# A tile's first and second attention units: values and place moved behind the next unit's scores time, in a bank of the h products

## The chip, the cores and the metric

The kernel runs on one core of a Trainium2 chip. Its time is the device time of one execution in microseconds (us). Engines: TensorE (PE, with its weight loads PEld), VectorE (DVE), ScalarE (ACT), GpSimd (POOL) and SyncE (SP), which issues nearly all transfers.

## The reference

Three layers on float32 data, 3072 tokens (4 batches of 768) of width 512 (8 heads of 64):

```python
# attention by chunks of 32 queries: 16 keys to the left, 8 to the right, and 8 memory keys
scores = scale * np.matmul(q_c, k_full.transpose(0, 1, 3, 2))
scores = scores - np.max(scores, axis=-1, keepdims=True)
a = np.exp(scores)
a = a / (np.sum(a, axis=-1, keepdims=True) + 1e-09)
out[:, :, c_start:c_end] = np.matmul(a, v_full)
# x = the heads side by side, [3072, 512]
h = x @ w_in                                              # 512 -> 2048
g = np.maximum(h, 0.0) + np.log1p(np.exp(-np.abs(h)))     # softplus
x = g @ w_out                                             # 2048 -> 512
out = ((x @ w_a) * (x @ w_b)) @ w_out2                    # 512 -> 1536 -> 512
```

## The kernel before, in words

**Stage 1** makes attention and the softplus layer, in 8 tiles (t = 0 to 7) of 384 tokens, about 74 us each, from 49 to 628 us of the span. A tile has 16 steps f, one for each 128 of the 2048 hidden columns. A step is `emit_h` (12 matmuls of 128x384 into a PSUM tile `ph`, tag "h", two banks), `emit_soft` (ScalarE Abs, Exp, Ln into `e`; VectorE `g`, L558, the last reader of `ph`; ScalarE and GpSimd split g into `gh` and `gl`), and `emit_x1` of the step two before (12 matmuls into four accumulators `px`, which hold four banks). Matmul inputs are split in a high and a low part, so a product takes three matmuls.

**Attention of tile t+1** is woven into tile t, in three units of 128 tokens (`Unit`, UPT = 3). A unit's steps: `turn` (VectorE transposes `kn`, `qn` into `kt`, `qt`), `scores` (32 small matmuls into two PSUM tiles `sc`, tag "att", two banks), `soft` and `norm` (softmax), `flip` and `flip2` (VectorE transposes the weights into `af`), `values` (32 small matmuls `pxa` of `af` with the values tile `vn`, one bank, tag "att"; the first 16 use the first half of the 128 queries, the rest the second), `place` (ScalarE copies `pxa` into the tile's x, VectorE subtracts for the low part). Tile 7 has no attention woven in.

**What sets the order.** `plan` is a list of (time, unit, step). Tile t has 32 times, two to an f: `att_at(slot)` is called behind `emit_h` and behind `emit_x1`, and pops each step whose time is at most the slot. A unit's `values` and `place` come at its time `at` less 0.1 and `at`; the others earlier, by STEPS (FIRST_STEPS for a tile's first unit, EARLY_STEPS for the three units woven into tile 0). In tiles 1 to 6 the program order is kept on TensorE, VectorE and SyncE; ScalarE and GpSimd are ordered by a scheduler.

**Loads.** There is one values tile (SETS = 1): the load for the next unit (`load_v`, two to five transfers on SyncE in pieces of 256 bytes) can start when the `values` before have read it. `Loaded.fetch` brings `kn` and `qn` of the tile after, in four parts (36 transfers, rows of 128 bytes), once the last unit of a tile has been turned. SyncE's other transfers in these tiles are weights on their way to scratch memory (`raw_*`, `v_scratch`) and results of the tile (`x_scratch`). All go out in the order of the program on one queue.

Stage 2 (628 to 1175 us) is the gated layer; the diff does not touch it.

Of the kernel before, what the change touches and what calls it, by code (L numbers as in the profile page):

```python
# [9 lines left out]
F32 = mybir.dt.float32  # L10
# [15 lines left out]
SETS = 1  # L26
# [24 lines left out]
def attn_moe_moe2(ctx: ExitStack, tc: tile.TileContext, q, k, v, mem_k, mem_v,  # L51
# [7 lines left out]
    P = 128  # L59
# [6 lines left out]
    UPT = TT // QU  # L66
# [4 lines left out]
    KT = DM // P  # L71
# [6 lines left out]
        name=nc.get_next_instruction_name(), act_func_set_id=6, ins=[], outs=[]))  # L78
# [8 lines left out]
    ps = ctx.enter_context(tc.tile_pool(name="ps", bufs=2, space=PSUM))  # L87
# [18 lines left out]
    class Weight:  # L106


        def __init__(self, dst, key):
            self.dst, self.key = dst, key  # L110
# [199 lines left out]
    class Block:  # L310
# [48 lines left out]
        def values(self):  # L359
            self.px = px = self.psum(4, "pxb")[:, :KT * QB].rearrange("p (i t) -> p i t", i=KT)  # L360
            for i in range(KT):
                for j in range(2):
                    r = slice(64 * j, 64 * j + 64)
                    nc.tensor.matmul(px[r, i], lhsT=self.vn[:, 2 * i + j, :], rhs=self.af[:, i, r], start=True, stop=True)
# [28 lines left out]
    class Unit:  # L393


        def __init__(self, u):
            self.u = u
            self.b, self.n = divmod(u, NU)

        def load_v(self):  # L400
            self.v = vsets[self.u % SETS]
            self.v.fetch(self.b, self.n)
# [66 lines left out]
        def values(self):  # L469
            u = self.u  # L470
            vn = self.v.v
            self.px = px = ps.tile([P, 512], F32, tag="att", name=f"pxa{u}").rearrange("p (i t) -> p i t", i=KT)

            for w in range(2):
                for i in range(KT):
                    for j in range(2):
                        nc.tensor.matmul(px[64 * j:64 * j + 64, i, QB * w:QB * w + QB], lhsT=vn[:, w, 2 * i + j],  # L477
                                         rhs=af[:, 2 * w:2 * w + 2, KT * j + i], start=True, stop=True)
# [18 lines left out]
    blocks = [Block(u) for u in range(BPT)]  # L497
    units = [Unit(u) for u in range(B * NU)]

    plan = []  # L500
    for i, unit in enumerate(units[UPT:]):
        at = 2 * NF1 * (i + 1) // UPT - START + NEXT_LATER * (i == EARLY) - (i % UPT == UPT - 1)
        steps = FIRST_STEPS if i % UPT == 0 else STEPS
        if i < EARLY:
            steps = EARLY_STEPS[i]
            at = steps[-1][0]
        plan += [(at + d - steps[-1][0], i, getattr(unit, step)) for d, step in steps]
        if i < SETS:
            plan.append((2 + i, -1, unit.load_v))
        if i + SETS < len(units[UPT:]):  # L510
            plan.append((at + 1, i, units[UPT + i + SETS].load_v))
        if i % UPT == UPT - 1 and unit.u + 1 < len(units):
            turned = at + steps[0][0] - steps[-1][0]
            plan += [(turned + 1 + part, i, partial(loaded.fetch, unit.u // UPT + 1, part)) for part in range(KT)]
# [549 lines left out]
```

## Time and profile before

| | us |
|---|---|
| median of 3 runs (lowest, highest) | 1179.31 (1178.32, 1180.07) |
| the profiled execution | 1176.61 |
| its span | 1174.8 |
| TensorE busy | 1165.4 |
| VectorE, ScalarE, GpSimd busy | 725.7, 532.2, 264.8 |

The span runs from the first to the last instruction of the profiled execution; the rest of its time lies around the span. A share of the whole span mixes the two stages, so the stretches of single tiles say more: tile t of stage 1 lies at 49 + 74 t to 123 + 74 t, roughly. Starts of matmuls on TensorE's timeline are exact, their ends are modelled and overlap the next start, so costs there are read from start to start.

### The profile page before, as it was taken

To read this page: it belongs to the slowest core of one execution; us is meant where nothing else is said; L and a number is where in the kernel's file an instruction comes from. 1 tells how busy PE (TensorE), PEld (TensorE's weight loads), DVE (VectorE), ACT (ScalarE), POOL (GpSimd) and SP (SyncE) were. 2 spreads that over 40 slices of the span, in tenths; PEclk is the share of its full clock that TensorE was granted. 3 is DMA by queue.
4 is the path that set the end of the run, shared out by engine and by line. 5 is a ranking of instruction groups with operands and counts; after the bars stand their busy time and mean duration, and the time that the engine had idled before them with its cause. 6 is when DMAs were issued, how large, how long until landed. Compare 5 with 4: busy or idle time off the path is not lost.

```text
span 1174.8 us, 20105 instructions
## 1 busy us (share of the span) xinstructions
PE 1165.4 (99%) x7462; PEld 1048.8 (89%) x7462; DVE 725.7 (62%) x1603; ACT 532.2 (45%) x1293; POOL 264.8 (23%) x239
## 2 busy tenths in 40 slices
PE   9899999999999999999999999999999999999998
PEld 6799999999999999999999888888888888888887
DVE  6888654556545665456377667867456657545555
ACT  6799666656566566665565332222211113111110
POOL 2000322323223222232233665721002101000000
PEclk9999999999999999999999999999999999999999
DMA  9965334353443534442374758464864443864301
GB/s 230 281 206 105 96 102 109 102 103 88 107 94 120 104 88 107 93 121 66 122 259 162 291 215 286 169 225 140 334 214 146 151 145 99 309 225 153 137 1 72
DMA packets 191154, 181.45 MB, mean 154 GB/s; under 512 B 120609, under 2 KB 149201, under 8 KB 191057
## 3 DMA queue, kind: packets, MB, share of 16 engines
q1 hardware_dynamic: 190672, 180.12, 49.2%
q8 instruction: 59, 0.97, 0.3%
q14 instruction: 39, 0.31, 0.1%
q0 software_dynamic: 384, 0.05, 0.0%
HBM read 129.79 MB, written 50.33 MB: 153 GB/s over the span
## 4 chain that ended last, share of the span: by engine, by line
PE 95%; DMA 2%; SPq 1%; ACT 0%; DVE 0%; issue 0%
PE px L571 23%; PE ph L547 22%; PE py L779 17%; PE pX L756 8%; PE pW L756 8%; PE pV L756 8%; PE pY L756 4%; PE pxa L477 2%; PE sc L430 1%; DMA kp<-in_k_dram 1%; DMA raw<-in_moe_w_in_dram 1%; SPq L331 1%; SPq L328 0%; PE sc L305 0%; PE pa L466 0%; SPq L102 0%
## 5 line engine op out<-in xcount | busy, mean ns | idle before, releaser
L547 PE MATMUL ph<-x,w 128*128 128x384 f32 x1536 | 289.7, 336 | 0.1
L571 PE MATMUL px<-gh,w 128*128 128x384 f32 x1024 | 283.2, 337 | 0.0
L547 PEld LDWEIGHTS ph<-x,w 128*128 128x128 f32 x1536 | 266.7, 188 | 2.2 <-issue 0.3
L779 PE MATMUL py<-w2o,c 128*128 128x512 f32 (+1 forms) x870 | 218.0, 388 | 0.0
L558 DVE SCALAR_TENSOR_TENSOR g<-ph,e 128x384 f32<-128x384 f32 x128 | 71.3, 557 | 206.3 <-ACT e L556 205.9
L779 PEld LDWEIGHTS py<-w2o,c 128*128 128x128 f32 x870 | 162.7, 188 | 33.5
L571 PEld LDWEIGHTS px<-gh,w 128*128 128x128 f32 x1024 | 186.7, 188 | 2.4 <-issue 0.2
L571 PE MATMUL px<-gl,w 128*128 128x384 f32 x512 | 171.2, 334 | 0.0
L838 ACT CAST c<-r 128x512 fp32r<-128x512 f32 x36 | 22.4, 621 | 308.2 <-DVE r L836 287.2
L538 POOL TENSOR_TENSOR gl<-g,gh 128x384 fp32r<-128x384 f32 x96 | 98.9, 1030 | 243.4 <-ACT gh L535 216.5
L554 ACT ACTIVATE e<-ph 128x384 f32<-128x384 f32 x128 | 62.2, 486 | 105.1 <-PE ph L547 91.0
L788 DVE TENSOR_TENSOR y<-py,y 128x512 f32<-128x512 f32 (+1 forms) x121 | 82.9, 685 | 36.2 <-PE py L779 36.0
L535 ACT CAST gh<-g 128x384 fp32r<-128x384 f32 x128 | 65.7, 513 | 73.8 <-DVE g L558 72.6
L571 PEld LDWEIGHTS px<-gl,w 128*128 128x128 f32 x512 | 96.1, 188 | 0.1
L448 DVE STREAM_TRANSPOSE af<-sm 32x256 f32<-32x256 f32 x180 | 78.2, 434 | 2.5
L555 ACT ACTIVATE e<-e 128x384 f32<-128x384 f32 x128 | 67.3, 526 | 4.0
L556 ACT ACTIVATE e<-e 128x384 f32<-128x384 f32 x128 | 67.3, 526 | 3.8
L835 DVE TENSOR_TENSOR d<-pW,q 128x512 f32<-128x512 f32 x36 | 24.9, 691 | 69.1 <-PE pW L756 69.1
L384 ACT ACTIVATE sm<-sm,st 128x96 f32<-128x96 f32 x168 | 60.5, 362 | 3.6 <-DVE st L380 3.6
L756 PE MATMUL pX<-x,u 128*128 128x512 f32 x216 | 54.8, 389 | 0.0
L756 PE MATMUL pW<-xs,u 128*128 128x512 f32 x216 | 54.8, 389 | 0.0
L756 PE MATMUL pY<-xs,u 128*128 128x512 f32 x216 | 54.8, 389 | 0.0
(162 smaller groups left out, 1636.7 us busy)
## 6 DMA issues: line engine op xcount, KB each, us to landing
u<-u_scratch SPq DMA_DIRECT2D x72, 512.0 KB
u_scratch<-u SPq DMA_DIRECT2D x36, 512.0 KB
w2o<-w2o_scratch SPq DMA_DIRECT2D x24, 512.0 KB
raw<-in_moe_w_in_dram SPq DMA_DIRECT2D x16, 512.0 KB
raw<-in_moe_w_out_dram SPq DMA_DIRECT2D x16, 512.0 KB
vn<-in_v_dram SPq DMA_DIRECT2D x35, 176.0 KB
raw_a<-in_moe_w_a_dram SPq DMA_DIRECT2D x12, 512.0 KB
raw_b<-in_moe_w_b_dram SPq DMA_DIRECT2D x12, 512.0 KB
```

The source lines that it names most:

```text
L448: nc.vector.transpose(out=af[32 * kb:32 * kb + 32, x], in_=self.sm[32 * x:32 * x + 32, :, 32 * kb:32 * kb + 32])
L535: anchor[0] = nc.scalar.copy(hi, val)
L538: engine.tensor_tensor(lo, val, hi.bitcast(F32), ALU.subtract)
L547: nc.tensor.matmul(ph, lhsT=w[:, a, kt * P:(kt + 1) * P], rhs=x[:, c, kt, :], start=n == 0, stop=n == 3 * KT - 1)
L554: nc.scalar.activation(e, ph, AF.Abs)
L555: nc.scalar.activation(e, e, AF.Exp, scale=-1.0)
L556: nc.scalar.activation(e, e, AF.Ln, bias=1.0)
L558: nc.vector.scalar_tensor_tensor(g, ph, 0.0, e, ALU.max, ALU.add)
L571: nc.tensor.matmul(acc[t][i][:, :TT], lhsT=a, rhs=c, start=f == 0 and m == 0, stop=f == NF1 - 1 and m == 2)
L756: nc.tensor.matmul(bank[:, :T2], lhsT=u[:, j, a, kt * P:kt * P + P], rhs=x[kt][:, c], start=first_ and m == 0, stop=m == 3 * KH - 1, skip_ ...
L779: nc.tensor.matmul(b, lhsT=c[:, x, r], rhs=w[:, y, cols], start=n == 0, stop=n == 3 * GROUP - 1)
L788: tt(y, b, y, ALU.add)
```

## The change

For a tile's first and second unit (i % UPT 0 and 1) `values` and `place` leave the unit's own times and take times just ahead of the next unit's `scores` (0.02 and 0.01 earlier). Their `pxa` comes from tag "h" in place of "att". The load of the next unit's values, which must follow, moves from `at + 1` to `at + 3` for these units. A tile's last unit keeps its times, its bank and `at + 1`.

```diff
--- before.py
+++ after.py
@@ -396,6 +396,7 @@
         def __init__(self, u):
             self.u = u
             self.b, self.n = divmod(u, NU)
+            self.own_bank = False
 
         def load_v(self):
             self.v = vsets[self.u % SETS]
@@ -469,7 +470,7 @@
         def values(self):
             u = self.u
             vn = self.v.v
-            self.px = px = ps.tile([P, 512], F32, tag="att", name=f"pxa{u}").rearrange("p (i t) -> p i t", i=KT)
+            self.px = px = ps.tile([P, 512], F32, tag="h" if self.own_bank else "att", name=f"pxa{u}").rearrange("p (i t) -> p i t", i=KT)
 
             for w in range(2):
                 for i in range(KT):
@@ -497,18 +498,23 @@
     blocks = [Block(u) for u in range(BPT)]
     units = [Unit(u) for u in range(B * NU)]
 
-    plan = []
+    plan, scored = [], {}
     for i, unit in enumerate(units[UPT:]):
         at = 2 * NF1 * (i + 1) // UPT - START + NEXT_LATER * (i == EARLY) - (i % UPT == UPT - 1)
         steps = FIRST_STEPS if i % UPT == 0 else STEPS
         if i < EARLY:
             steps = EARLY_STEPS[i]
             at = steps[-1][0]
-        plan += [(at + d - steps[-1][0], i, getattr(unit, step)) for d, step in steps]
+        whens = [(at + d - steps[-1][0], step) for d, step in steps]
+        scored[i] = dict((step, a) for a, step in whens)["scores"]
+        if i % UPT and i > 0:
+            plan += [(scored[i] + d, i - 1, getattr(units[UPT + i - 1], step)) for d, step in ((-0.02, "values"), (-0.01, "place"))]
+            units[UPT + i - 1].own_bank = True
+        plan += [(a, i, getattr(unit, step)) for a, step in whens if step not in ("values", "place") or i % UPT == UPT - 1]
         if i < SETS:
             plan.append((2 + i, -1, unit.load_v))
         if i + SETS < len(units[UPT:]):
-            plan.append((at + 1, i, units[UPT + i + SETS].load_v))
+            plan.append((at + 1 if i % UPT == UPT - 1 else at + 3, i, units[UPT + i + SETS].load_v))
         if i % UPT == UPT - 1 and unit.u + 1 < len(units):
             turned = at + steps[0][0] - steps[-1][0]
             plan += [(turned + 1 + part, i, partial(loaded.fetch, unit.u // UPT + 1, part)) for part in range(KT)]
```

TensorE, tile 1, the values of unit 7 (`pxa7`) and the scores of unit 8 (`sc0_8`), which is the tile's last unit. Before:

```order
L547 MATMUL ph1_10_2226<-x1_1059,w18_1143 128x384 x12
L477 MATMUL pxa7_2246<-af_83,vn0_82 64x64 x16
L571 MATMUL px1_0_1864<-gh_666,w19_1195 128x384
...
L430 MATMUL sc0_8_2303<-kt8_2219,qt8_2220 64x96 x2
L430 MATMUL sc1_8_2304<-kt8_2219,qt8_2220 64x96 x2
...
L547 MATMUL ph1_11_2321<-x1_1059,w20_1236 128x384 x12
```

After:

```order
L577 MATMUL px1_3_1867<-gh_666,w19_1193 128x384
L577 MATMUL px1_3_1867<-gl_667,w19_1193 128x384
...
L478 MATMUL pxa7_2282<-af_83,vn0_82 64x64 x16
L431 MATMUL sc0_8_2301<-kt8_2219,qt8_2220 64x96 x2
L431 MATMUL sc1_8_2302<-kt8_2219,qt8_2220 64x96 x2
```

The values stood behind a ph and ahead of a block of px; now they stand behind that block, with the scores directly after them. It is the same in tile 0 for both units and in tiles 1 to 3 for both.

TensorE, tile 4, the values of unit 16 and the scores of unit 17. Before:

```order
L547 MATMUL ph4_10_4722<-x4_3652,w18_1143 128x384 x12
L477 MATMUL pxa16_4742<-af_83,vn0_82 64x64 x16
L571 MATMUL px4_0_4365<-gh_666,w19_1195 128x384
...
L547 MATMUL ph4_11_4804<-x4_3652,w20_1236 128x384 x12
L430 MATMUL sc0_17_4824<-kt17_4715,qt17_4716 64x96 x2
```

After:

```order
L577 MATMUL px4_3_4368<-gh_666,w19_1193 128x384
L478 MATMUL pxa16_4782<-af_83,vn0_82 64x64 x16
L553 MATMUL ph4_11_4801<-x4_3690,w20_1236 128x384 x12
L431 MATMUL sc0_17_4821<-kt17_4715,qt17_4716 64x96 x2
L431 MATMUL sc1_17_4822<-kt17_4715,qt17_4716 64x96 x2
```

Here a block of ph stays between values and scores: 0.02 takes the values into the slot before that of the scores. It is the same for both units of tiles 4, 5 and 6.

SyncE, tile 1: the load of the last unit's values (`vn`), among the kn and qn transfers for the next tile. Before:

```order
L188 DMA kn_78<-in_k_dram 32x12x32
L190 DMA qn_79<-in_q_dram 32x12x32
L214 DMA vn0_82<-in_v_dram 88x8x64 x2
L673 DMA v_scratch<-val_b1_2300 128x512
...
L190 DMA qn_79<-in_q_dram 32x12x32
L214 DMA vn0_82<-in_v_dram 88x8x64 x2
L655 DMA raw_o1_2595<-in_moe2_w_out_dram 128x1024
```

After:

```order
L190 DMA qn_79<-in_q_dram 32x12x32
L679 DMA v_scratch<-val_b1_2279 128x512
L188 DMA kn_78<-in_k_dram 32x12x32
...
L190 DMA qn_79<-in_q_dram 32x12x32
L214 DMA vn0_82<-in_v_dram 88x8x64 x4
L661 DMA raw_o1_2595<-in_moe2_w_out_dram 128x1024
```

Before, the first `vn` row (the tile's last unit) had 20 of the 36 kn and qn transfers ahead of it and 16 behind; the second (the next tile's first unit) stood behind them all. After, both stand behind them all, as one row of four transfers. It is the same in tiles 2 to 5; in tile 6 there is nothing left to fetch for kn and qn.

## Rows read from the trace of the kernel before

**Rows 1.** The page: TensorE's busy line, the chain that ended last.

```profile
PE 1165.4 (99%) x7462; PEld 1048.8 (89%) x7462; DVE 725.7 (62%) x1603; ACT 532.2 (45%) x1293; POOL 264.8 (23%) x239
...
PE 95%; DMA 2%; SPq 1%; ACT 0%; DVE 0%; issue 0%
```

**Rows 2.** Busy time in tile 2: PE, PEld, DVE, ACT, POOL, clock, DMA, GB/s.

```profile
193.00:267.00 74.00, 74.00 (x578) 71.93 (x577) 41.32 (x128) 45.77 (x126) 20.85 (x20) 1.00 0.41 101
```

**Rows 3.** TensorE's timeline, tile 3: start, us, engine, line, tiles, count.

```profile
362.10 0.34 PE L571 MATMUL px<-gh,w 128*128 128x384 f32 x1
362.37 1.15 PE L477 MATMUL pxa<-af,vn 96*64 96x64 f32 x32
363.45 2.35 PE L547 MATMUL ph<-x,w 128*128 128x384 f32 x12
...
369.90 0.89 PE L430 MATMUL sc<-kt,qt 64*64 64x96 f32 x32
370.72 0.44 PE L571 MATMUL px<-gh,w 128*128 128x384 f32 x1
371.00 0.34 PE L571 MATMUL px<-gl,w 128*128 128x384 f32 x1
```

**Rows 4.** The same in tile 1: second unit's values, last unit's scores.

```profile
165.90 1.22 PE L477 MATMUL pxa<-af,vn 96*64 96x64 f32 x32
...
169.36 1.08 PE L430 MATMUL sc<-kt,qt 64*64 64x96 f32 x32
```

**Rows 5.** Timelines of VectorE and TensorE around a values step, tile 4.

```profile
390.06 0.56 DVE L558 SCALAR_TENSOR_TENSOR g<-ph,e 128x384 f32<-128x384 f32 x1 [0.31 <-ACT e L556]
...
390.98 2.24 PE L547 MATMUL ph<-x,w 128*128 128x384 f32 x12
```

**Rows 6.** SyncE's queue of transfers in tile 1: start, us, issues.

```profile
178.47 0.91 SPq L214 DMA_DIRECT2D vn<-in_v_dram  x2
179.47 0.90 SPq L673 DMA_DIRECT2D v_scratch<-val_b  x1
...
189.30 0.57 SPq L190 DMA_DIRECT2D qn<-in_q_dram  x1
190.02 0.86 SPq L214 DMA_DIRECT2D vn<-in_v_dram  x2
```

**Rows 7.** TensorE's timeline: the last unit's values in tiles 1 to 5.

```profile
189.29 1.22 PE L477 MATMUL pxa<-af,vn 96*64 96x64 f32 x32
...
263.17 1.22 PE L477 MATMUL pxa<-af,vn 96*64 96x64 f32 x32
...
337.06 1.22 PE L477 MATMUL pxa<-af,vn 96*64 96x64 f32 x32
...
410.82 1.22 PE L477 MATMUL pxa<-af,vn 96*64 96x64 f32 x32
...
484.52 1.22 PE L477 MATMUL pxa<-af,vn 96*64 96x64 f32 x32
```

**Rows 8.** SyncE's queue: the last qn of the burst, tiles 2 to 5.

```profile
262.00 0.47 SPq L190 DMA_DIRECT2D qn<-in_q_dram  x1
...
337.26 0.47 SPq L190 DMA_DIRECT2D qn<-in_q_dram  x1
...
409.54 0.47 SPq L190 DMA_DIRECT2D qn<-in_q_dram  x1
...
484.58 0.47 SPq L190 DMA_DIRECT2D qn<-in_q_dram  x1
```

**Rows 9.** The view of transfers: us from issue to landing stand last.

```profile
mem_n<-in_mem_k_dram POOLq DMA_DIRECT2D x12, 4.0 KB, 3.3
```

**Rows 10.** The view of transfers, 193.5 to 200 us: packets by size.

```profile
DMA packets 116, 0.42 MB, mean 65 GB/s; under 512 B 16, under 2 KB 16, under 8 KB 115
```

**Rows 11.** Busy time, 44 to 47 us, columns as in rows 2.

```profile
44.00:47.00 3.00, 1.32 (x21) 0.87 (x19) 2.90 (x7) 2.94 (x7) 0.00 (x0) 1.00 0.78 273
```

## The prediction

> **What bounds the kernel now.** I read the page's busy line and its chain of waits first: TensorE is busy for 1165.4 of the 1174.8 us, and the chain that ends last runs through it for 95% of the span [rows 1]. Then the table of stretches for one tile of the first stage: 74.00 of 74.00 us busy [rows 2], and all six tiles in which the moved steps lie look the same. So TensorE is the limit there, nothing that only shortens another engine's work can show, and everything that makes TensorE wait is paid in full. Two questions are left: what the moved matmuls cost TensorE where they stand now and where they will stand, and whether their operands will be there. The first is read from TensorE's timeline, the second from the issue times on the DMA queue of SyncE.
>
> **What an insert costs.** In [rows 3] a wide matmul follows the one before it after 0.17 us in the steady state. Around the values (pxa) the starts are 362.10 (the last px), 362.37 (pxa), 363.45 (ph): 0.27 until the small matmuls begin instead of 0.17, then 1.08 for the 32 of them with their drain. Around the scores (sc) they are 369.90 (sc), 370.72 (px), 371.00 (next px): 0.82 for the 32, and then 0.28 instead of 0.17 for the first wide one. Every separate insert thus pays about 0.10 on entry and 0.11 at its end. Where values and scores stand back to back, one entry and one end go: 0.21 us a pair. A change from one tile height to another inside the pair might cost a drain; the pxa to px step has one already, so I charge nothing more.
>
> **Gains, part by part.** The change moves the values of 14 units. (a) In tiles 1 to 3 six of them come to stand directly ahead of scores, as the order shows for pxa7: 6 x 0.21 = 1.3 us. In tiles 4 to 6 the other six do not: the plan's times there fall into different slots, and pxa16 is followed by a whole ph before the scores come. They stay separate inserts, 0 gained. In tile 0 two merge, but ScalarE also converts weights there and what feeds these values ends late, so I count nothing, give or take 0.4. (b) The second scores of tiles 1 to 3 last 1.08 where the others last 0.89 [rows 3, 4]: 0.19 of wait inside, since the "att" bank that the second score tile takes is still being emptied by the place step. With the values in an "h" bank that goes: 3 x 0.19 = 0.6. (c) The second unit's values last 1.22 instead of 1.15 in each of six tiles [rows 3, 4], since the second half waits for its transposes; later values find them done: 6 x 0.07 = 0.4. Together 2.3 us.
>
> **The borrowed bank.** After moved values the next ph takes the bank of the ph before, so it needs that step's g. The nearest existing case is [rows 5]: a ph starts at 390.98, while the g that reads the one before ended at 390.06 + 0.56 = 390.62, 0.36 earlier, with one pxa between the two. That is the distance the rows of tiles 4 to 6 will have; merged pairs have 0.8 more. I take 0; if VectorE's extra work falls in front of that g, it is at most 0.3 for some of 14, bound 2 us.
>
> **The loads: where it is lost.** The change also moves a load. The values tile vn is one single set, so the load for a tile's last unit can be issued only after the values of its second unit, and it goes two plan slots later than before. In the SyncE order the 36 kn and qn transfers of the next tile lie exactly there: before, vn stood in the middle of them; after, it stands behind the last one. SyncE issues one about each 0.5 us, and the burst already ends as the last unit's values come up. In tile 1 vn was issued at 178.47, the last qn at 189.30 for 0.57, so until 189.87 [rows 6], and TensorE began the last unit's values at 189.29 [rows 7]. TensorE works in order, and px and ph stand behind the values: nothing hides a wait.
>
> Working for tile 1. Taking vn out of the burst's middle gives back 179.47 - 178.47 = 1.0 us [rows 6]; so vn is issued at 189.87 - 1.0 + 0.1 = 188.97. The second of its two transfers is issued 0.5 later. How long from issue to landing no row of vn says; the bounds are: the next vn, issued at 190.02, still had 16 small packets moving after 193.5 [rows 6, 10], 3.5 us and more after issue; the one kind of transfer that the view gives a landing time for, 4 KB, took 3.3 [rows 9]. I take 3.3 from the second issue: it lands at 188.97 + 0.5 + 3.3 = 192.8. The second half of the values needs it; without a wait that half would start at 189.29 + 0.58, less 0.47 that TensorE gains in this tile after the burst begins (0.21 + 0.19 + 0.07) = 189.4. Wait: 3.4 us. The same sum elsewhere, with the ends of the burst from [rows 8] (start of the last qn + 0.47) and the starts from [rows 7]:
> - tile 2: three transfers for vn, so 1.5 given back and 1.0 until the last issue. 262.47 - 1.4 + 1.0 + 3.3 = 265.4, against 263.17 + 0.58 - 0.47 = 263.3: 2.1 us
> - tile 3: 337.73 - 0.9 + 0.5 + 3.3 = 340.6, against 337.2: 3.4 us
> - tile 4: 410.01 - 1.4 + 1.0 + 3.3 = 412.9, against 410.82 + 0.58 - 0.12 = 411.3: 1.6 us
> - tile 5: 485.05 - 0.9 + 0.5 + 3.3 = 487.95, against 484.52 + 0.58 - 0.07 = 485.0: 2.9 us
> Tile 6 has no kn and qn to load, tile 0 had its vn outside the burst and ahead of it by the order; both 0. Sum 13.4 us. The lower bound: the writes to v_scratch that stood behind vn took up to 0.90 [rows 6], and could fall to the 0.47 of its neighbours, 0.4 in each of three tiles, and the landing could be 0.5 shorter in all five: 13.4 - 1.2 - 2.5 = 9.7. The upper bound: the burst gives nothing back because the engines, not the issues, set its pace: five times 1.0 to 1.5 more, 19.
>
> The Trainium skill ("DMA: Bandwidth & Descriptors", "Rules for kernel authors") says to issue a transfer early and wait for it late, so that its fixed cost lies under work; this change does the opposite for vn, and it speaks against it. Its "Anatomy of one DMA" gives about 2.0 us plus bytes over 436 GB/s for one; my estimate from that is 2.4 us for 176 KB, and the five waits would be 4.5 us less, 8.9; the packets after 193.5 [rows 10] contradict it, so the sum does not use it.
>
> **Sum.** -2.3 + 13.4 = +11.1 us. The profiled execution took 1176.61, span 1174.8 and 1.8 around it; the changed one would take 1187.7. The median of the runs shown is 2.7 above the profiled execution, so 1190.4 us.
>
> **Rivals.**
> (A) The other side: faster. vn lands in time. For that it would have to be issued before about 185.5 in tile 1, or the burst to end 3.4 us earlier than I put it. For it: the transfers move fewer bytes than the engines could. Against: 17 transfers at 0.5 us stand between its old place and its new one, and the queue issues in order. Then only the gains stay: 1179.3 - 2.3 = 1177.0. It decides at a wait of under 0.46 us a tile (2.3 / 5). 5%.
> (B) The clock. Five idle stretches of about 3 us on TensorE that did not exist. In this trace the granted clock stays at 1.00 (2.4 GHz) even over 44 to 47 us, where it was idle for 1.68 of 3.00 [rows 11]; no row has a longer gap. If it fell to 1.2 GHz for as long again as each wait lasted, half of that time is lost: 13.4 / 2 = 6.7 more, 1197. The Trainium skill ("TensorE: Matmul & The Clock Gate", Part 1) has an idle array fall to the lower clock; the row here, with its short gap, neither shows nor excludes it for these. 8%.
> (C) Shorter waits: landing as the lower bound and a faster burst, 9.7 - 2.3 = +7.4, 1186.7, or less, if SyncE catches up further. 14%.
> (D) The change does less than it says (six of twelve pairs do not meet) and the borrowed bank costs up to 2 us with the same loads: 1192.5. 8%.
> The forecast itself, 1190.4 with 1188.5 to 1192: 65%.
>
> **How the numbers follow.** Range 1185.0 to 1195.5: forecast, (C) and (D), without most of (A) and (B). A difference of 0.2%, 2.4 us, is about what a measurement of this kernel can tell from none. Faster by more than that holds half of (A): 0.03; within it the other half and a (C) with waits of a third of mine: 0.05; slower 0.92.
>
> **What would show it.** Right: in tiles 1 to 5 TensorE idle for 1.5 to 3.5 us in front of or inside the last pxa of the tile, put down to the vn transfer; vn issued right after the last qn; no such idle time in tile 6; pxa directly before sc in tiles 1 to 3, and sc at 0.89. Wrong: TensorE still busy for 74.00 of 74.00 in these tiles (A), a granted clock under 1.00 after the waits (B), waits under 1 us in all (C), idle time of ph before L553 put down to g (D).

## The result and the profile after

The changed kernel takes 1193.44 us (median of 4 runs, 1192.11 to 1196.38), the kernel before, run beside it, 1179.36 (4 runs): ratio 1.012, 95% interval 1.010 to 1.014, so 14.1 us slower. The forecast was 1190.4, range 1185.0 to 1195.5. Of all executions below one, the profiled one of e6, took 2407.99 us where its others took 1206.62 to 1210.35, and no number is read from it.

The page of the changed kernel: busy line, granted clock in 40 slices, and the chain that ended last (it answers to [rows 1]).

```profile
PE 1170.3 (98%) x7462; PEld 1054.7 (88%) x7462; DVE 726.3 (61%) x1603; ACT 532.7 (45%) x1293; POOL 263.7 (22%) x239
...
PEclk9999999999989999999999999999999999999999
...
PE 81%; SPq 8%; DMA 4%; DVE 3%; ACT 3%; issue 1%; DVEq 0%
```

The chain, 95% TensorE before, now runs for 8% through SyncE's queue and for 4% through transfers. The issues of kn and qn make 5% of it (L188 2%, L190 3%): their burst has come onto the path. What TensorE waited for between 119 and 580 us (engine and line, what it waited for, us in all, times, longest):

```profile
PE pxa L478 <- DMA vn<-in_v_dram: 12.2, 6, 3.7
```

This is the only wait, and before there was none. Its place in tile 1, first on SyncE's queue, then on TensorE's timeline (answers to [rows 6] and [rows 7]):

```profile
191.31 0.46 SPq L190 DMA_DIRECT2D qn<-in_q_dram  x1
191.88 5.50 SPq L214 DMA_DIRECT2D vn<-in_v_dram  x4
197.47 0.44 SPq L661 DMA_DIRECT2D raw_o<-in_moe_w_out_dram  x1
```

```profile
189.97 2.24 PE L553 MATMUL ph<-x,w 128*128 128x384 f32 x12
195.21 1.84 PE L478 MATMUL pxa<-af,vn 96*64 96x64 f32 x32 [3.00 <-DMA vn<-in_v_dram]
196.98 0.69 PE L577 MATMUL px<-gh,w 128*128 128x384 f32 x1
```

vn leaves behind the last qn, 0.3 us before TensorE wants it, and the first values start 195.21 - 191.88 = 3.3 us after the issue. The next row of px lasts 0.69, not 0.45: the clock has fallen. By stretch, for tiles 1, 2 and 3 (columns as in [rows 2], the clock stands third from the end):

```profile
190.00:195.00 5.00, 2.21 (x13) 1.89 (x11) 3.09 (x7) 2.05 (x4) 1.01 (x1) 1.00 0.62 121
195.00:200.00 5.00, 4.79 (x44) 4.61 (x45) 2.23 (x4) 1.33 (x4) 1.00 (x1) 0.66 0.44 112
...
274.00:278.00 4.00, 4.00 (x16) 4.00 (x15) 2.54 (x5) 0.99 (x4) 3.14 (x5) 0.57 0.75 180
...
351.00:356.00 5.00, 4.90 (x41) 4.62 (x42) 2.02 (x4) 1.33 (x4) 1.00 (x1) 0.50 0.42 101
```

A clock of 0.50 is 1.2 GHz, half of the 2.4 of a clock of 1.00. The clock of a stretch is its mean, so the time lost in a stretch is its length times one less the clock: 5 x 0.34 = 1.7, 4 x 0.43 = 1.7, 5 x 0.50 = 2.5, together 5.9 us.

To put the terms together I measure each tile from its first scores to those of the next tile, and the rest up to the last px of stage 1. That leaves out the start of the kernel, which is not the change's: the first scores of tile 1 come at 123.4 to 129.9 us in the seven profiles measured so (those of the table, e5 and e7), 125.12 in before and 128.61 in after, because a wait of 1.68 us at 45 to 47 us became one of 3.20 and the clock fell behind it. Stage 2 is 538.4 us in all of them.

| us | tile 1 | 2 | 3 | 4 | 5 | 6 and 7 | sum |
|---|---|---|---|---|---|---|---|
| before | 69.69 | 73.90 | 75.95 | 73.77 | 73.70 | 144.32 | 511.3 |
| after | 73.72 | 77.18 | 81.48 | 75.38 | 75.61 | 144.25 | 527.6 |
| e1b (the load mended) | 69.05 | 73.23 | 75.31 | 73.63 | 73.63 | 144.22 | 509.1 |
| e2 (the load moved alone) | 73.53 | 77.42 | 80.59 | 76.21 | 77.00 | 144.29 | 529.0 |
| e3b (and all pairs) | 69.07 | 73.23 | 75.29 | 73.23 | 73.23 | 143.88 | 507.9 |
| waits for vn in after | 3.00 | 2.08 | 3.71 | 1.69 | 1.76 | 0 | 12.2 |
| waits for vn in e2 | 2.29 | 1.83 | 2.79 | 2.32 | 1.55 | 0 | 10.8 |

After less before is 16.3 us, and it comes apart as -2.2 (e1b less before) + 12.2 of waits + 6.3 left over, of which the rows above show 5.9 as low clock.

### The profile page after: what moved, and what is told of

The parts are those of the page before. It is cut to its first block, busy times and chain, and to the rows that moved or that the text cites. A ratio compares the mean times of both kernels' runs of the same rounds, so it can differ in the third digit from the quotient of the medians.

```text
span 1194.6 us, 20100 instructions
## 1 busy us (share of the span) xinstructions
PE 1170.3 (98%) x7462; PEld 1054.7 (88%) x7462; DVE 726.3 (61%) x1603; ACT 532.7 (45%) x1293; POOL 263.7 (22%) x239
## 4 chain that ended last, share of the span: by engine, by line
PE 81%; SPq 8%; DMA 4%; DVE 3%; ACT 3%; issue 1%; DVEq 0%
PE px L577 17%; PE py L785 16%; PE ph L553 16%; PE pX L762 8%; PE pW L762 8%; PE pV L762 8%; PE pY L762 4%; SPq L190 3%; SPq L188 2%; PE pxa L478 2%; DMA vn<-in_v_dram 1%; DMA raw<-in_moe_w_in_dram 1%; DMA kp<-in_k_dram 1%; SPq L331 1%; PE sc L431 1%
## 5 line engine op out<-in xcount | busy, mean ns | idle before, releaser
L762 PE MATMUL pX<-xa,u 128*128 128x512 f32 x216 | 54.8, 389 | 0.0
```

The source lines that it names most:

```text
L762: nc.tensor.matmul(bank[:, :T2], lhsT=u[:, j, a, kt * P:kt * P + P], rhs=x[kt][:, c], start=first_ and m == 0, stop=m == 3 * KH - 1, skip_ ...
```

## Experiments

**The load alone.** e2: the kernel before with one edit.

```diff
-            plan.append((at + 1, i, units[UPT + i + SETS].load_v))
+            plan.append((at + 1 if i % UPT == UPT - 1 else at + 3, i, units[UPT + i + SETS].load_v))
```

> The kernel before with nothing changed but the time of that load (at + 3 for a tile's first and second unit). Theory L: the waits for vn appear without the moved steps; TensorE arrives 0.5 us later in tiles 1 to 3, so some 10.7 us of waits, and 4 to 6 us of low clock behind them: 1194 to 1196 us. Rival M: within 1 us of the kernel before, 1179.4.

1192.72 us (1191.85 to 1193.83), ratio 1.0129 (1.0105 to 1.0152) to the kernel before, 1177.84 beside it. What TensorE waited for:

```profile
PE pxa L477 <- DMA vn<-in_v_dram: 6.2, 3, 2.8
PE pxa L477 <- DVE g L558: 4.6, 2, 2.3
```

Together 10.8 us, against 10.7 expected. The two put down to g (tiles 1 and 4) are the same wait: a g happens to end just as these values start, but in tile 5 the same values start at 499.60 while the g of that place still runs (499.78 to 500.34), so they do not need it. In all five tiles they start 3.2 to 4.1 us behind vn's issue. So 14.9 us come from moving one load, with no matmul moved; the 1194 to 1196 expected was counted from 1179.4. By the tiles e2 takes 17.7 us more than before, 10.8 of waits and 6.9 beyond them, and the change as a whole 16.3. It is hardly better, although the moved steps gain 2.2 (e1b below): its waits add up to 12.2, since TensorE reaches the same wait earlier.

**The load mended.** e1 was meant to keep the moved steps and bring vn forward, and e3 to make all pairs meet as well.

> The change with its load of the last unit's values placed behind the first of the four parts of kn and qn, and so ahead of 24 transfers in place of behind them. Theory L (the late load is the whole loss): no wait for vn in front of a pxa, granted clock 1.00 from tile 1 on, and what is left is the gain of the moved steps, 2.3 us: 1179.4 - 2.3 = 1177.1 us, 1176.0 to 1178.2. Rival M (the moved steps or the borrowed bank cost it): still 1185 us or more, with the waits for vn gone.

> The kernel of e1_vn_behind_first_part with values and place taking the very time of the scores, so that the six pairs of tiles 4 to 6 stand together as well. By the working on inserts, 0.21 us a pair: 1.3 us under e1, about 1175.9 us. Rival: the borrowed bank's g (its spare time is larger for a merged pair) or a drain between the two tile heights takes it back: no difference from e1, 1177.

They took 1210.2 and 1202.31 us. The fault was mine: my time for the load also applied to a tile's middle unit, whose vn then arrived ahead of the first unit's values, which read the wrong unit's rows and waited for them. They say nothing on either theory. With that time for the last unit's load alone, and with the other three parts of kn and qn held back until it is out, e1b:

```diff
-            plan.append((at + 1 if i % UPT == UPT - 1 else at + 3, i, ...load_v))
+            plan.append((at + (1 if i % UPT == UPT - 1 else 2.36 if i % UPT == 1 and i > EARLY else 3), i, ...load_v))
-            plan += [(turned + 1 + part, i, partial(loaded.fetch, ...
+            plan += [(turned + 1 + part if part == 0 or i < EARLY else turned + 3.8 + 0.1 * part, i, partial(loaded.fetch, ...
```

> The change with the load of a tile's last values placed behind the first of the four parts of kn and qn (tiles 1 to 5), so ahead of 24 transfers; in e1 a second load, that of the middle unit, had slipped ahead of the values that still had to be read. Theory L (the late load is the whole loss): no wait for vn, granted clock 1.00 from tile 1 on, and 2.3 us under the kernel before, which these runs put at 1177.8: 1175.5 us, 1174 to 1177. Rival M (moved steps or borrowed bank cost time): 1185 us or more without waits for vn.

1174.1 us (12 runs) against 1176.15 (23 runs): ratio 0.9976, interval 0.9963 to 0.9989, so 2.8 us faster, 1.3 to 4.4 (the medians lie 2.0 apart). TensorE's rows for the pair of tile 1 (answers to [rows 4]), and the stretch of tiles 1 to 6:

```profile
170.58 1.15 PE L478 MATMUL pxa<-af,vn 96*64 96x64 f32 x32
171.66 0.89 PE L431 MATMUL sc<-kt,qt 64*64 64x96 f32 x32
172.48 2.38 PE L553 MATMUL ph<-x,w 128*128 128x384 f32 x12
```

```profile
120.00:560.00 440.00, 440.00 (x3455) 428.95 (x3453) 249.29 (x761) 277.93 (x759) 127.03 (x121) 1.00 0.41 100
```

TensorE never waits, the clock stays at 1.00, values last 1.15 where they lasted 1.22 and scores 0.89 where they lasted 1.08. Theory L holds, M falls: with the load mended the moved steps and the borrowed bank cost nothing, and by the tiles they gain 2.2 us, where 2.3 was worked out.

**All pairs meet.** e3b: e1b with values and place at the scores' own time.

```diff
-            plan += [(scored[i] + d, i - 1, ...) for d, step in ((-0.02, "values"), (-0.01, "place"))]
+            plan += [(scored[i], i + d, ...) for d, step in ((-1, "values"), (-0.5, "place"))]
```

> e1b_vn_behind_first_part with values and place at the very time of the scores, so that the pairs of tiles 4 to 6 meet too. Inserts: 6 x 0.21 = 1.3 us under e1b, 1174.2 us. Rival (g of the borrowed bank or a drain takes it back): no difference from e1b. In the profile: the merged pair of tile 4 costs TensorE 0.2 us less than pxa and sc apart, or the same.

1173.55 us, ratio 0.9978 (0.9964 to 0.9992) to before: from e1b the times can't tell it. The tiles can: 73.63 becomes 73.23 in tiles 4 and 5, 144.22 becomes 143.88 in the last, 1.1 us in all or 0.19 a pair, where 0.21 was expected. The pair in tile 4:

```profile
387.85 1.15 PE L478 MATMUL pxa<-af,vn 96*64 96x64 f32 x32
388.93 0.89 PE L431 MATMUL sc<-kt,qt 64*64 64x96 f32 x32
389.75 0.45 PE L577 MATMUL px<-gh,w 128*128 128x384 f32 x1
```

Values to scores takes the same 1.08 us as values to ph did [rows 3] (rows of tile 4, by their times, not of tile 3): no drain is added.

**The clock.** Theory C (not the prediction's rival (C)) is that the time lost beyond the waits is the low clock behind them. First the wait was to be filled with matmuls that nobody reads (e6), then the same with sizes that fit (e7). The edit of e7, in parts (one unit is 128 columns; e6 had 9, 6, 11, 5 and 5, each times four):

```diff
+COVER = {5: 13, 8: 9, 11: 16, 14: 7, 17: 7}
+        if i in COVER:
+            plan.append((at - 0.15, i, partial(warm, COVER[i], mem_n.rearrange("p i s -> p (i s)"))))
```

> The change itself, with matmuls that nobody reads put ahead of the last unit's values in tiles 1 to 5 (9, 6, 11, 5, 5 of 512 columns, about 0.3 us each, all shorter than the wait that stands there). The wait is then spent working. Theory C (behind the three longest waits the clock is low and costs 1.6 + 1.7 + 2.5 = 5.8 us on top of the 12.2 us of waits): the time falls by some 5.8 us, to 1187.6, 1186 to 1189, with granted clock 1.00 in tiles 1 to 5. Rival (only the waits count): 1193.4, or more by what the extra matmuls overrun.

1208.5 us (1206.62 to 1210.35): the filling was longer than the waits. One such matmul takes not 0.3 us but 0.88 (in tile 3 of e7 four of them, two rows of the trace each, stand from 345.04 to 348.56), so the 36 of e6 take some 32 us against 12.2 of waits. It decided nothing.

> The covered wait with sizes that fit (in e6 each 512-column matmul took two passes and 0.85 us in all, 31 us over five waits of 12): now 13, 9, 16, 7 and 7 columns of 128, 0.213 us each, so 2.8, 1.9, 3.4, 1.5 and 1.5 us ahead of the last values of tiles 1 to 5. Theory C: no idle stretch over 0.5 us, no low clock in tiles 1 to 5, and 5.8 us under the change: 1187.6, 1186 to 1189. Rival: low clock costs nothing extra: 1193.4.

1186.28 us (1185.41 to 1192.43), ratio 1.0088 (1.0066 to 1.011). From 119 to 500 us, all but the end of its fifth tile:

```profile
119.00:500.00 381.00, 379.72 (x2899) 364.83 (x2894) 210.78 (x639) 234.75 (x639) 106.47 (x102) 1.00 0.41 100
```

The clock stays at 1.00 and TensorE is idle for 1.3 us in all. TensorE works through the waits it had, and still, from its first scores in tile 1 to the end of stage 1, it takes 522.4 us, 5.2 less than the change: 6.1 less in tiles 1 to 3, where the clock had fallen, and 0.9 more in tiles 4 and 5, where it had not. So theory C holds: about 5 to 6 us of the loss is the clock, the rest the waits.

**A dose.** e5: vn ahead of the last two of the 36 transfers (the main line of its edit).

```diff
+            plan += [(turned + KT + d, i, partial(loaded.fetch, unit.u // UPT + 1, KT - 1, rows)) for d, rows in ((0, (0, 1, 2)), (0.3, (3,)))]
```

> The change with the load of the last unit's values ahead of the last two of the 36 transfers in place of behind them. The dose: two issues at 0.5 us, so each wait 1.0 us shorter: 12.2 - 5 = 7.2 us of waits. Theory C (the low clock comes with the longer waits): the clock stays at 1.00 behind the waits of tiles 1 and 2 (now 2.0 and 1.1 us) and falls at most in tile 3 (2.7), so 5.0 + 3.3 = 8.3 us less than the change: 1185.1. Only waits, no price of the clock: 1188.4. If the burst were paced by something else than issues: no change, 1193.4.

1187.59 us, but from 1183.68 to 1193.92 in four runs, with mean clocks from 0.999 to 0.993: in some runs the clock is low for longer than in others. In the profiled one (1183.68) the waits add up to 7.8 us (7.2 expected), and the clock fell behind one of five, that of tile 3 (2.1 us):

```profile
186.00:196.00 10.00, 7.75 (x89) 7.03 (x92) 4.70 (x10) 3.54 (x9) 2.03 (x2) 1.00 0.60 146
...
342.00:346.00 4.00, 4.00 (x15) 4.00 (x15) 2.23 (x4) 0.82 (x4) 1.00 (x1) 0.57 0.76 204
```

Two issues fewer ahead make each wait 0.9 us shorter on average (12.2 to 7.8 in five), about the 1.0 that follows if the issues set the pace. The median does not tell the two columns of the expectation apart.

**The borrowed bank.** e4b: e3b without own_bank.

```diff
-            units[UPT + i - 1].own_bank = True
```

> e3b_all_pairs_meet with pxa of all units from tag att again, so that it is seen what the borrowed bank is worth once values stand ahead of scores. The two score tiles then need both att banks, one of which holds pxa until place has read it: ScalarE 0.58 and VectorE 0.68 us, and the drain and waits for a turn on both engines, with the scores' 0.82 us alternating between both banks. Theory: 1.3 to 2.5 us of wait in front of sc for each of 12 pairs (tiles 1 to 6) and less in tile 0, 16 to 30 us over e3b: 1190 to 1204. Rival (the place is quick enough, the bank is a detail): within 3 us of e3b, 1173.6.

1217.34 us (1214.15 to 1220.66), ratio 1.0338, 42 us over before (1175.61 beside it; 40 by the ratio), more than the 16 to 30 expected over e3b. Waits:

```profile
PE sc L431 <- DVE x L486: 19.5, 12, 2.3
PE sc L305 <- DVE x L486: 6.5, 2, 3.7
```

26.0 us are waits, inside the expectation, though tile 0 has 6.5 of them, where less was expected. Most of the rest is the clock again: its mean is 0.985 over 1218.9 us, so (1 - 0.985) x 1218.9 = 18.3 us lost. The bank is what makes the order back to back possible: without it that order loses 42 us on before, with it it gains 2.6.

## Why the prediction was right, and where it was off

- **The path.** Right. TensorE is the limit, and the only new wait on it is the one forecast: vn behind the burst, in tiles 1 to 5, none in tile 6.
- **The waits.** 13.4 forecast, 12.2 measured: 3.4, 2.1, 3.4, 1.6, 2.9 against 3.00, 2.08, 3.71, 1.69, 1.76. Tile 5 is the one that was off. There the burst gave back 1.1 us more than the 1.0 of vn: vn left 1.4 us ahead of TensorE's arrival, not 0.3. Half of the 1.1 is the v_scratch write (0.98 in before, 0.41 in after), whose cheaper form I had left to the lower bound, half a single kn issue (1.83 and 1.36).
- **Issue to landing.** From vn's first issue to the first values 3.3 us pass in tile 1, 3.0 to 3.7 in the five tiles; in tile 5 it is 3.0 to the first half and 3.9 to the second. The 3.8 of the sum (0.5 + 3.3) fits. One of the two bounds under it was misread, though: the 16 small packets after 193.5 [rows 10] are not vn's. Transfers of 256 and 512 KB come with some 16 small packets each in this trace (487 for 30 of them between 900 and 1000 us), one of 512 KB stood behind vn (raw_o, issued at 190.97), and between 193.5 and 194 there is no small packet at all. vn's had ended by 193.5, 3.5 us behind its first issue, so the row bounds the landing from above and not from below. The fit of the Trainium skill ("DMA: Bandwidth & Descriptors", "Anatomy of one DMA") is stated for transfers that GpSimd issues; the estimate from it, 2.4 us, is too short for these, which go out from SyncE. The Trainium skill ("DMA: Bandwidth & Descriptors", "Rules for kernel authors") has a transfer issued early and waited for late; the change does the opposite for vn, and the 12.2 us of waits agree.
- **The gains.** 2.3 forecast, 2.2 measured by the tiles (e1b), 2.8 by the runs. Merged pairs, the bank wait of the scores and the transposes' wait are each as put. The pairs that do not meet gained nothing, as the order showed, and 0.19 each once they met. Tile 0 gained nothing, as put: less the wait near 45 us, the first scores of tile 1 come at 123.44 in before, 123.41 in e3b and 123.21 in e5.
- **The borrowed bank.** 0 forecast; TensorE does not wait for g in front of a ph in any of these tiles. Rival (D) falls.
- **The mis-sized term: the clock.** The sum charged it at nothing, and (B) stood apart as a rival with 8% and 6.7 us. It is no rival but a part of the price: behind three of five waits the clock fell, 5.9 us by the rows, 5.2 by e7. A granted clock under 1.00 behind the waits stood among the prediction's own signs of being wrong, and it came. My evidence against it [rows 11] was one gap of 1.68 us, shorter than four of the five waits I forecast. The Trainium skill ("TensorE: Matmul & The Clock Gate", Part 1) says that an idle array falls to the lower clock: the waits of 3.00, 2.08 and 3.71 us agree, those of 1.69 and 1.76 left it at 1.00. With that term the sum is -2.3 + 13.4 + 5.9 = 17.0, and the tiles show 16.3.
- **From profile to median, and luck.** The measured 14.1 lies closer to my 11.1 than the 16.3 of the tiles, because the runs take in the wait near 45 us, which varies by itself. The profiled before was 2.75 us under its median, the profiled after 2.94 over its own, and their first scores of tile 1 stood 3.49 apart; if the starts alone make these differences, as an estimate, the median runs differ by 16.3 + 3.49 - 2.75 - 2.94 = 14.1. Against the kernel before as it ran beside the experiments (1177.84, 1176.15 and 1175.61) the change costs 15.6 to 17.8. At 16.3 over 1179.36 the time would have been 1195.7, just above the range. That it fell inside, with 5.9 us left out of the sum, is partly luck, and it lies above the 1188.5 to 1192 that got 65%.

## What to carry to other kernels

When a step moves, look at what its buffers free: here two plan slots on one load, in the midst of a burst on an in-order queue, cost eight times what the moved matmuls gained (12.2 + 5.9 against 2.2), and moving the load ahead of 24 of the burst's 36 transfers turned the loss into a gain. Price a new wait on a busy TensorE at its length and, where the clock falls behind it, half of the time at the low clock on top. An order that depends on a time 0.02 ahead of a computed one should be read in the program's order, since rounding may put a whole step between: by the plan's sums the scores come at 117.0 in tile 3, in one slot with values 0.02 earlier, and at 139.00000000000003 in tile 4, one slot behind them.

## What the runs showed of the hardware

- **The clock and the length of a wait.** It fell behind waits of 3.00, 2.08 and 3.71 us (after) and stayed behind 1.69 and 1.76; but in e2 it fell behind one of 1.55 (tile 5) and stayed behind one of 2.32 (tile 4), and in e5 it stayed behind 2.17 (tile 1). Length alone does not decide it, and what does stays open. A fall cost 1.5 to 1.9 us beyond the wait, whatever the wait was (e2 against before, after against e1b), and 2.5 where the clock stayed low longer (tile 3 of after). e2's tile 4, behind its 2.32 us, and its tile 5, behind its 1.55:

```profile
424.19 1.34 PE L477 MATMUL pxa<-af,vn 96*64 96x64 f32 x32 [2.32 <-DVE g L558]
426.00:427.00 1.00, 1.00 (x8) 1.00 (x7) 0.80 (x2) 0.58 (x2) 0.35 (x1) 1.00 0.67 151
...
499.60 1.37 PE L477 MATMUL pxa<-af,vn 96*64 96x64 f32 x32 [1.55 <-DMA vn<-in_v_dram]
501.00:505.00 4.00, 4.00 (x14) 4.00 (x15) 2.23 (x4) 1.33 (x4) 1.01 (x1) 0.57 0.78 204
```

- **A mean clock as a price.** (1 - mean clock) x span gives about the time lost to it. In e4b it is 18.3 us, with 26.0 us of waits and 3.1 near 45 us 47.4; its span is 49.2 longer than that of e3b, whose clock is 1.000. In e2 it is 7.1, against 6.9 beyond the waits by the tiles.
- **A wait early in the span**, near 45 us, lasts from nothing (e3b) to 4.31 us (e7) in the profiles. Where it lasts up to 1.68 us, the first scores of tile 1 come later by about that wait (123.41 without it, 125.12 with 1.68). Behind 2.69, 3.20 and 4.31 us (e1b, after, e7) the clock falls, and they come 1.8 to 2.1 us later still. That makes up to 6.4 us between executions, more than the moved steps are worth. What decides the wait was not tried.
